# Hedgehog linear attention plus a Mish layer on one core: per-head weights loaded by rows and spread by TensorE, and a new order of the head of the program

## The chip, the cores and the metric

The kernel runs on one core of one Trainium2 chip. The metric is the device time of one execution in microseconds (us), as the median of several runs. Before the change it is 173.7 us: three runs gave 173.72, 173.63 and 173.70.

## What is computed

The input x has 2048 tokens of 512 features. Each token is normalised (layer norm without weights), and two branches start from the normalised tokens xn: a linear attention with 32 heads of 16 features, and a dense layer of 512 -> 1792 -> 512 with Mish. The result is x plus both.

```python
q, k, v = split_heads(xn @ wqkv)                 # 32 heads of 16
pq, pk  = q @ w_phi[h], k @ w_phi[h]             # 16 x 16 weights of each head
phi     = concat(softmax(p), softmax(-p))        # for q and for k
kv, z   = sum_s phi_k * v, sum_s phi_k
A       = ((phi_q @ kv) / (phi_q @ z + 1e-6)) @ wo
B       = mish(xn @ w1 + b1) @ w2
out     = x + A + B
```

## The kernel before

Everything is bf16 in SBUF; products go through PSUM, whose first six banks hold one 128x512 tile each. Tokens come in 16 tiles of 128, four to a group. Two weights of the attention are multiplied together on the chip first: the 512x512 weights of the keys, and w_phi as a block-diagonal matrix. The product, `wkp`, gives the logits pk from xn in one projection. That product is needed before the first logits can be made, so the head of the program (everything before the large stream of matmuls) has two strands that meet in `first_logits` (L197):

- Tokens: the first two tiles of x are loaded (L477), their mean and variance taken on VectorE (`first_stats`, L549), the inverse root made on GpSimd or on ScalarE (`first_root`, L553), the tile normalised on VectorE (`first_apply`, L562), turned by TensorE (`first_turn`, L566) and copied to `xnT` (`first_keep`, L587).
- Weights: the keys' weights come in two ways. Their last two blocks of 128 rows are turned by the DMA (L483, into `wT`). The first two are loaded as they are (L482, into `wkp`), turned on TensorE by matmuls with an identity (`turn_keys`, L573, tile `ptw`) and copied to `wT` by ScalarE (`keep_keys`, L581). w_phi is loaded into `wsrc` (L488) with row 16 i + a of a partition block holding row a of head i; a partition receives four runs of 16 elements. `weights_by_block` (L527) multiplies it with the mask `block` on VectorE to `Wbd`, the block-diagonal matrix. `fold` (L147) multiplies `wT` with `Wbd` into the tile `pfold`, four matmuls for each of the four blocks of 128 rows, and `unfold` (L159) copies each block to `wkp`.

`first_logits` takes the four blocks of `wkp` in order, each with both tiles of tokens (8 matmuls, tile `pl`). Behind it stands `value` (L209), the projection to v with the weights `wv`, and then the rest: logits of the other tokens, the hidden layer (`hidden`, L218), Mish on ScalarE (`mish`, L231), softmax work on VectorE and ScalarE, the key-value sums, the queries, the output.

The order of all work is written out by hand: `STEPS` (L24) is a list of short names with arguments, `run` (L627) maps each name to a function, and each engine executes its instructions in the order in which the steps issue them; semaphores make one engine wait for another. `H 3 @5` is hidden unit 3 into PSUM bank 5, `M 3` its Mish, `LC 0 2 a` the copy of a tile of logits by ScalarE, `v` stands for VectorE, `p` for GpSimd. The loads of the head stand in front of the list (L477 to L493) and go out on two queues: SyncE's (SP) and ScalarE's. Ahead of everything TensorE does 12 dummy matmuls on constants (L519), nine of 512 columns and three of 128; `WARM, SHORT = 9, 3`. GpSimd makes the constants: the identity `ident`, the mask `block`, `mhalf`, `eps` and the ones in `vext` (L496 to L508).

Of the kernel before, what the change touches and what calls it, by code (L numbers as in the profile page):

```python
# [22 lines left out]
WARM, SHORT = 9, 3  # L23
# [3 lines left out]
@4,5; LS 2; LS 3; RS 2 a; LC 0 0 a; V 1 @1; RS 3 p; AZ 2; TP 2 @2; TC 2 a; VC 1 a; AM; V 0 @3; LC 0  # L27
1 v; AZ 3; CB; TP 3 @4; TC 3 v; L 0 2 @5; LC 0 2 a; H 0 @0; M 0; L 0 3 @2; LC 0 3 a; H 1 @1; M 1; H
2 @4; M 2; H 3 @5; H 4 @0; H 5 @2; VC 0 a; H 6 @1; M 3; M 4; M 5; H 7 @4; M 6; M 7; H 8 @3; H 9 @5;
H 10 @0; M 8; H 11 @2; H 12 @1; LN 1; M 9; E 0 0; AP 1 0; AP 1 1; H 13 @4; L 1 0 @3; DX 3; L 1 3 @5;  # L30
DW 2; E 0 1; X 0 1; LN 2; LC 1 0 v; LC 1 3 v; WL 1; LN 3; AP 2 0; AP 2 1; X 0 0; V 6 @3; M 10; M 11;
M 12; H 14 @5; S 0 0; WL 2; LC 1 2 a; VC 6 a; M 13; AP 3 0; H 15 @0; H 16 @2; H 17 @1; LC 1 1 a; AP
3 1; WT; H 18 @3; H 19 @4; M 14; M 15; M 16; M 17; H 20 @5; M 18; M 19; H 21 @0; H 22 @2; H 23 @1; H
24 @3; M 20; M 21; H 25 @4; H 26 @5; M 22; M 23; H 27 @0; M 24; M 25; M 26; M 27; H 28 @2; M 28; H
29 @1; M 29; E 1 0; E 1 1; S 0 1; L 2 1 @3; L 2 0 @4; LC 2 0 v; L 2 2 @5; LC 2 1 v; L 2 3 @0; F 0
@2; R 0 0 a; L 3 2 @1; R 0 1 a; LC 2 2 v; LC 2 3 a; FC 0 a; X 1 0; F 1 @4; F 2 @3; FC 2 a; N 0 0; L
3 0 @5; V 9 @0; LC 3 0 a; V 3 @2; VC 3 a; LC 3 2 v; A 0 0; VC 9 a; V 7 @1; F 3 @3; V 2 @5; VC 7 a; V
8 @2; L 3 3 @0; FC 3 a; X 1 1; VC 2 a; FC 1 v; E 2 0; L 4 0 @4; DW 3; LC 3 3 a; E 2 1; V 4 @1; N 0
1; VC 8 v; X 2 0; S 1 1; LC 4 0 a; S 1 0; L 4 3 @3; VC 4 a; L 4 2 @5; V 11 @0; A 0 1; LC 4 2 a; V 5
@2; VC 11 a; R 1 1 a; S 2 0; L 4 1 @4; LC 4 1 a; L 3 1 @1; VC 5 a; LC 3 1 a; H 30 @5; H 31 @0; LC 4  # L40
3 v; R 1 0 a; M 30; H 32 @4; M 31; M 32; H 33 @2; M 33; N 1 1; H 34 @1; H 35 @3; H 36 @5; M 34; H 37
@0; M 35; H 38 @4; E 3 0; H 39 @2; H 40 @1; M 36; N 1 0; M 37; M 38; M 39; H 41 @3; H 42 @5; H 43
@0; M 40; A 1 0; M 41; E 3 1; M 42; M 43; A 1 1; X 2 1; V 12 @4; VC 12 a; L 5 0 @2; V 10 @1; V 15
@3; VC 15 a; V 13 @5; V 14 @0; E 4 0; E 4 1; LC 5 0 a; VC 13 v; VC 10 a; L 5 2 @4; X 3 1; X 3 0; L 6
3 @3; VC 14 a; L 5 3 @2; O 0 @5; LC 5 2 a; S 2 1; S 3 1; S 3 0; R 3 1 a; R 2 1 a; N 2 1; R 2 0 a; L
6 0 @1; R 3 0 a; N 3 0; L 5 1 @0; LC 5 1 a; N 3 1; O 1 @4; L 6 1 @0; LC 6 0 a; LC 6 3 a; L 6 2 @1; H
44 @3; X 4 0; N 2 0; S 4 0; LC 6 2 a; LC 6 1 v; LC 5 3 a; A 2 0; A 2 1; A 3 0; A 3 1; H 45 @1; X 4
1; M 44; W 4 0 v; H 46 @2; H 47 @0; M 45; M 46; S 4 1; M 47; KV; H 48 @3; M 48; H 49 @1; H 50 @2; M
49; H 51 @0; H 52 @3; M 50; M 51; Q 0 0; H 53 @1; G 0 0; H 54 @2; M 52; Q 0 1; H 55 @0; W 4 1 v; L 7
3 @3; M 53; M 54; E 5 0; G 0 1; L 7 0 @1; E 5 1; Q 1 0; C 0 a; O 2 @2; G 1 0; LC 7 0 a; X 5 0; Q 1  # L50
1; O 3 @1; G 1 1; E 6 0; S 5 0; P 0; P 1; C 1 a; LC 7 3 a; W 5 0 v; L 7 2 @3; M 55; Y 0; O 4 @0; O 5
@5; P 2; LC 7 2 a; Y 1; X 5 1; Q 2 0; G 2 0; L 7 1 @4; E 6 1; LC 7 1 a; P 3; S 5 1; Y 2; W 5 1 v; X
6 0; Q 2 1; G 2 1; O 6 @3; O 7 @2; E 7 0; C 2 a; S 6 0; Y 3; W 6 0 a; E 7 1; Q 3 0; O 8 @4; P 4; Y
4; G 3 0; X 6 1; Q 3 1; G 3 1; X 7 0; S 6 1; C 3 a; O 9 @1; P 5; X 7 1; W 6 1 v; Q 4 0; G 4 0; O 10
@0; Y 5; Q 4 1; G 4 1; S 7 0; C 4 a; O 11 @5; W 7 0 v; Q 5 0; G 5 0; P 6; P 7; Q 5 1; G 5 1; Y 6; O
12 @3; S 7 1; C 5 a; Q 6 0; W 7 1 a; P 8; P 9; G 6 0; Q 6 1; Y 7; Y 8; Y 9; G 6 1; O 13 @2; Q 7 0; C
6 v; G 7 0; P 10; P 11; Y 10; Q 7 1; O 14 @4; G 7 1; P 12; C 7 a; Y 11; Y 12; P 13; OH 0 @1; P 14;
PH 0; OH 1 @0; PH 1; Y 13; Y 14; YH 0; YH 1
# [4 lines left out]
def kernel(  # L63
# [29 lines left out]
    wphi_v = A_w_phi.rearrange("(j i) a b -> (i a) j b", j=4)  # L93
# [18 lines left out]
    wsrc = wts.tile([P, 4, DH], BF16, name="wsrc")  # L112
    wv = wts.tile([P, KT, D], BF16, name="wv")
# [8 lines left out]
    ident = consts.tile([P, P], BF16, name="ident")  # L122
    mhalf = consts.tile([P, TPG], FP32, name="mhalf")
# [9 lines left out]
    tables = ["natural_log_exp_and_others"]  # L133
# [343 lines left out]
    for t in range(2):  # L477
        nc.sync.dma_start(x_sb[:, t, :], x_v[:, t, :])  # L478
# [4 lines left out]
    nc.sync.dma_start_transpose(  # L483
        out=wT_of[0][:, :, 2 * P : 4 * P], in_=A_wqkv[2 * P : 4 * P, D : 2 * D]
    )
    nc.scalar.dma_start(b1b[:], b1_v[:, :])
    with nc.allow_non_contiguous_dma(reason="tiny w_phi load"):
        nc.scalar.dma_start(wsrc[:], wphi_v)  # L488
    nc.sync.dma_start(x_sb[:, 2:4, :], x_v[:, 2:4, :])
    nc.sync.dma_start(wv[:], wqkv_v[:, :, 2 * D : 3 * D])  # L490
    nc.sync.dma_start(w1_sb[:, :, 0 : 7 * P], w1_v[:, :, 0 : 7 * P])
    nc.sync.dma_start(x_sb[:, 4:8, :], x_v[:, 4:8, :])
    nc.sync.dma_start(w1_sb[:, :, 7 * P : F], w1_v[:, :, 7 * P : F])  # L493

    nc.scalar.preload_act_table_set(tables[0])
    make_identity(nc, ident[:])  # L496

    nc.gpsimd.memset(block[:], 1.0)
# [6 lines left out]
    nc.gpsimd.memset(mhalf[:], -0.5)  # L505
    nc.gpsimd.memset(eps[:], 1e-5)
# [12 lines left out]
    for n in (512,) * WARM + (P,) * SHORT:  # L519
        dummy(n)  # L520

# [5 lines left out]
    def weights_by_block():  # L527
        nc.vector.tensor_tensor(
            out=Wbd[:].rearrange("p j (h e) -> p j h e", h=8),
            in0=block[:, None, :, :].to_broadcast([P, 4, 8, 16]),  # L530
            in1=wsrc[:, :, None, :].to_broadcast([P, 4, 8, 16]),
            op=ALU.mult,
        )
# [19 lines left out]
    def first_root(i, on):  # L553
        _, mv, rstd = ln_of[0]
        r = rstd[:, i : i + 1]
        if on == "a":
            nc.scalar.activation(r, mv[:, i, 1:2], ACT.Ln, bias=eps[:])
            nc.scalar.activation(r, r, ACT.Exp, scale=-0.5)
        else:
            root(r, mv[:, i : i + 1, :])  # L560
# [26 lines left out]
    def first_keep(i, copy):  # L587
        copy(xnT[:, i, :, :], pf_of.pop(("t", i))[:].rearrange("p (k c) -> p k c", k=KT))
# [34 lines left out]
    def load_queries():  # L623
# [4 lines left out]
        "KM": masks, "AW": lambda: dummy(P), "WB": weights_by_block, "PB": bias,  # L628
# [52 lines left out]
```

## Time and profile before

| | us |
|---|---|
| median of three runs (lowest, highest) | 173.7 (173.63, 173.72) |
| span of the profiled execution, first to last instruction | 172.0 |
| the rest of the time, around the span | 1.7 |
| TensorE busy, of the span | 168.0 (98%) |
| VectorE busy | 143.9 (84%) |
| ScalarE busy | 123.8 (72%) |
| GpSimd busy | 7.8 (5%) |

The profile gives the profiled execution no time of its own beside its span, so the rest around the span is taken as the median less the span. All times inside the profile count from the start of that span. Engines are named PE (TensorE matmul), PEld (its weight loads), DVE (VectorE), ACT (ScalarE), POOL (GpSimd) and SP (the queue that issues most transfers). A row of the timeline has the start in us, the duration in us, the engine, the line and operation, the output and input, the shapes, how many instructions are merged in it (x2), and in brackets how long the engine stood idle before it and what ended that wait. Matmuls are pipelined: a row with eight of them lasts from the first one's start to the last one's end.

### The profile page before, as it was taken

To read this page: it belongs to the slowest core of one execution; us is meant where nothing else is said; L and a number is where in the kernel's file an instruction comes from. 1 tells how busy PE (TensorE), PEld (TensorE's weight loads), DVE (VectorE), ACT (ScalarE), POOL (GpSimd) and SP (SyncE) were. 2 spreads that over 40 slices of the span, in tenths; PEclk is the share of its full clock that TensorE was granted. 3 is DMA by queue.
4 is the path that set the end of the run, shared out by engine and by line. 5 is a ranking of instruction groups with operands and counts; after the bars stand their busy time and mean duration, and the time that the engine had idled before them with its cause. 6 is when DMAs were issued, how large, how long until landed. Compare 5 with 4: busy or idle time off the path is not lost.

```text
span 172.0 us, 2735 instructions
## 1 busy us (share of the span) xinstructions
PE 168.0 (98%) x1047; PEld 82.6 (48%) x1047; DVE 143.9 (84%) x223; ACT 123.8 (72%) x199; POOL 7.8 (5%) x23
## 2 busy tenths in 40 slices
PE   8899999999999999999999999999999999999993
PEld 2554444444454544454445644544444444554452
DVE  3869998999599999969989999799799998884333
ACT  2778899997999989889978989977282792432200
POOL 4123002300000000000000000000000000000000
PEclk9999999999999999999999999999999999999999
DMA  4997299589000000000000194309335618668941
GB/s 124 303 370 248 54 255 347 99 162 228 21 0 0 0 4 0 0 0 0 4 0 0 36 113 99 61 9 150 90 97 116 153 52 197 146 134 216 110 131 61
DMA packets 44185, 18.02 MB, mean 105 GB/s; under 512 B 35980, under 2 KB 44172, under 8 KB 44172
## 3 DMA queue, kind: packets, MB, share of 16 engines
q1 hardware_dynamic: 43472, 17.73, 43.9%
q8 instruction: 8, 0.13, 0.4%
q10 hardware_dynamic: 700, 0.12, 0.4%
q14 instruction: 5, 0.04, 0.1%
HBM read 7.10 MB, written 2.10 MB: 53 GB/s over the span
## 4 chain that ended last, share of the span: by engine, by line
PE 95%; DMA 2%; SPq 0%; ACT 0%; issue 0%; DVE 0%
PE po L457 28%; PE ph L223 28%; PE pl L189 14%; PE po L464 8%; PE pv L189 8%; PE pnd L412 2%; PE pkv L381 2%; DMA wkp<-in_A_wqkv_dram 2%; PE pl L204 1%; PE pfold L151 1%; PE pwide L189 1%; SPq L478 0%; PE ptr L569 0%; PE ptw L576 0%; ACT wT L582 0%
## 5 line engine op out<-in xcount | busy, mean ns | idle before, releaser
L457 PE MATMUL po<-w_sb,acts 128*128 128x512 bf16 (+2 forms) x238 | 50.8, 366 | 0.0
L223 PE MATMUL ph<-xnT,w_sb 128*128 128x512 bf16 x224 | 49.8, 379 | 0.0
L234 ACT ACTIVATE acts<-ph,b1f 128x512 bf16<-128x512 f32 x56 | 36.3, 701 | 4.2 <-PE ph L223 4.0
L300 DVE TENSOR_REDUCE s<-e 128x128 f32<-128x2048 bf16 x16 | 36.1, 2276 | 0.5 <-ACT e L283 0.5
L223 PEld LDWEIGHTS <-w_sb 128*128 128x128 bf16 x224 | 21.7, 98 | 25.7
L457 PEld LDWEIGHTS <-acts 128*128 128x128 bf16 x238 | 22.1, 98 | 23.6
L283 ACT ACTIVATE e<-e 128x2048 bf16<-128x2048 bf16 x16 | 30.5, 1919 | 0.0
L189 PEld LDWEIGHTS <-xnT 128*128 128x128 bf16 x184 | 17.5, 98 | 19.6
L471 DVE TENSOR_TENSOR x_sb<-po,x_sb 128x512 bf16<-128x512 f32 (+2 forms) x17 | 11.0, 656 | 8.4 <-PE po L464 8.4
L464 PE MATMUL po<-wqk,xnT 128*128 128x512 bf16 (+2 forms) x68 | 15.6, 366 | 0.0
L189 PE MATMUL pv<-wv,xnT 128*128 128x512 bf16 x64 | 15.6, 379 | 0.0
L189 PE MATMUL pl<-wqk,xnT 128*128 128x512 bf16 x64 | 15.4, 379 | 0.0
L427 ACT COPY ds<-pnd 128x32 f32<-128x32 f32 x16 | 2.9, 182 | 16.5 <-PE pnd L412 16.5
L247 ACT CAST p_sb<-pl 128x512 bf16<-128x512 f32 x21 | 12.2, 594 | 3.6 <-PE pl L189 3.4
L139 ACT ACT_TABLE_LOAD x10 | 12.8, 1283 | 0.2
L258 DVE TENSOR_TENSOR m<-m 128x512 bf16<-128x512 bf16 (+1 forms) x32 | 11.5, 359 | 1.1
L189 PE MATMUL pl<-wkp,xnT 128*128 128x512 bf16 x48 | 11.7, 379 | 0.0
L267 DVE TENSOR_TENSOR e<-p_sb,m 128x2048 bf16<-128x2048 bf16 x8 | 9.8, 1226 | 1.8 <-PE pkv L381 1.5
L258 DVE TENSOR_TENSOR m<-p_sb 128x1024 bf16<-128x1024 bf16 x16 | 10.9, 681 | 0.0
L165 DVE BATCH_NORM_STATS2 stats<-x_sb 128x6 f32<-128x512 bf16 x16 | 10.1, 677 | 0.9 <-DMA x_sb<-in_A_x_dram 0.9
L267 DVE TENSOR_TENSOR e<-m,p_sb 128x2048 bf16<-128x2048 bf16 x8 | 9.8, 1225 | 0.3
L334 DVE TENSOR_TENSOR e<-e,r 128x2048 bf16<-128x2048 bf16 x8 | 9.6, 1216 | 0.5 <-ACT r L309 0.5
(68 smaller groups left out, 133.9 us busy)
## 6 DMA issues: line engine op xcount, KB each, us to landing
w_sb<-in_B_w_dram SPq DMA_DIRECT2D x4, 896.0 KB, 7.8
out_dram<-x_sb SPq DMA_DIRECT2D x15, 128.0 KB, 1.8
x_sb<-in_A_x_dram SPq DMA_DIRECT2D x3, 512.0 KB, 7.5
wv<-in_A_wqkv_dram SPq DMA_DIRECT2D x1, 512.0 KB, 4.6
wqk<-in_A_wo_dram SPq DMA_DIRECT2D x1, 512.0 KB, 4.9
x_sb<-in_A_x_dram SPq DMA_DIRECT2D x2, 128.0 KB, 2.1
wkp<-in_A_wqkv_dram SPq DMA_DIRECT2D x1, 256.0 KB, 3.6
x_sb<-in_A_x_dram SPq DMA_DIRECT2D x1, 256.0 KB, 3.6
```

Source lines behind the costliest of these rows:

```text
L139: nc.scalar.preload_act_table_set(name)
L189: nc.tensor.matmul(pp, lhsT=xnT[:, t, kt, :], rhs=w[:, kt, :], start=(kt == 0), stop=(kt == KT - 1),)
L223: nc.tensor.matmul(ph_of[u][:], lhsT=w1_sb[:, kt, f * P : (f + 1) * P], rhs=xnT[:, g * TPG : (g + 1) * TPG, kt, :], start=(kt == 0), stop= ...
L234: nc.scalar.activation(acts[:, f, g * 512 : (g + 1) * 512], ph_of.pop(u)[:], ACT.Mish, bias=b1f[:, f : f + 1])
L247: copy(p_of[s][:, i, :], pl_of.pop((s, i)))
L258: nc.vector.tensor_tensor(out=m[:], in0=src[:, :, 0:half], in1=src[:, :, half : 2 * half], op=op)
L267: nc.vector.tensor_tensor(out=e_of[s][:].rearrange("p t j l c -> p (t j) l c")[:, :, pl, :].rearrange("p t (c e o) -> p t c e o", e=8, o=2 ...
L283: nc.scalar.activation(v, v, ACT.Exp)
L300: nc.vector.reduce_sum(t[:], pair(s, k).rearrange("p t j l (c e) -> p (t j l c) e", e=16), axis=AX.X)
L457: nc.tensor.matmul(po_of[t, c.stop][:, c], lhsT=acts[:, f, t * P : (t + 1) * P], rhs=w2_sb[:, f, c], start=(f == 0), stop=False,)
L464: nc.tensor.matmul(po_of[t, c.stop][:, c], lhsT=oT_of[t // 2][:, t % 2 * 4 + j, :], rhs=wo_sb[:, j, c], start=False, stop=(j == 3),)
L471: nc.vector.tensor_tensor(out=y, in0=po_of.pop((t, c.stop))[:, c], in1=y, op=ALU.add)
```

## The change

Five things change, all of them in the head.

1. w_phi is loaded by rows: `wraw` has in each partition four whole rows of 16 of one head, one run of 64 elements. A constant `sel`, a matrix of 0 and 1 kept in the memory of `kvm`, spreads them: 16 matmuls of 16 columns (`spread`) put the rows where `wsrc` has them, in a PSUM tile `pspread`, and VectorE copies that to `wsrc` (step `WC`).
2. The loads become steps (`D`), in a new order. ScalarE's queue carries the first tile of x and w_phi; SP's the second tile of x, the keys' weights in two loads of one block each, the turned blocks, tiles 2 and 3 of x, b1, and the rest. The third group's tokens go ahead of the second half of w1.
3. VectorE fills `ident`, `block`, `sel`, `eps` and `mhalf`; GpSimd only selects in them (`affine_select`).
4. The dummies become steps too (`AW`): five of 512 columns, one of 256 and two of 128 at the start, and two of 512 behind the turned keys' weights.
5. The steps of the head stand in another order, up to the first group's hidden units; from `H 13` on the list is as it was.

```diff
-KM; LS 0; RS 0 p; LS 1; RS 1 a; DX 2; PB @0; AZ 0; AZ 1; TW 0 @1; TW 1 @2; TP 0 @3; TP 1 @4; TK 0 a;
-TK 1 a; WB; F0 0 @5; FD 0 a; F0 1 @1; TC 0 v; F0 2 @2; F0 3 @3; FD 2 a; TC 1 v; FD 1 v; FD 3 a; LP i
+AW 512; AW 512; D x011 s; D wn01 s; AW 512; D wn12 s; AW 512; D x001 a; D phi a; AW 512; LS 0; AW
+256; AW 128; AW 128; WX @2; TL; TW 0 @1; RS 0 a; TK 0 a; TW 1 @4; LS 1; WC v; D wt1 s; AZ 0; KM; AW
+512; WB v; AW 512; D x022 s; RS 1 p; TP 0 @0; TK 1 a; F0 0 @5; AZ 1; TC 0 v; FD 0 a; F0 1 @2; TP 1
...
-    nc.sync.dma_start(wkp[:, 0:2, :], wqkv_v[:, 0:2, D : 2 * D])
-    nc.scalar.dma_start(b1b[:], b1_v[:, :])
-        nc.scalar.dma_start(wsrc[:], wphi_v)
...
+        elif what[:2] == "wn":
+            k = slice(int(what[2]), int(what[3]))
+            q.dma_start(wkp[:, k, :], wqkv_v[:, k, D : 2 * D])
...
+        elif what == "phi":
+            q.dma_start(wraw[:], A_w_phi.rearrange("h (c a) b -> (h c) (a b)", c=4))
...
+    nc.gpsimd.affine_select(
+        out=sel, in_=sel, pattern=[[1, 4 * P + 4]], compare_op=ALU.not_equal,
+        fill=1.0, base=-3, channel_multiplier=-4,
+    )
...
-    for n in (512,) * WARM + (P,) * SHORT:
-        dummy(n)
...
+    def spread(b):
+
+        pf_of["x"] = bank(b, "pspread")
+        for j in range(4):
+            for a in range(4):
+                nc.tensor.matmul(
+                    pf_of["x"][:, j * DH : (j + 1) * DH],
+                    lhsT=sel[:, j * P + 3 - a : (j + 1) * P + 3 - a],
+                    rhs=wraw[:, a * DH : (a + 1) * DH],
+                    start=(j == 0 and a == 0), stop=(a == 3), skip_group_check=True,
+                )
...
+        "WC": lambda c: copies[c](wsrc[:].rearrange("p j b -> p (j b)"), pf_of.pop("x")[:, 0 : 4 * DH]),
```

Three places show what the new list does to the engines.

VectorE between the statistics of the second tile and those of the third; before (`xn` is a normalised tile, `Wbd` the block-diagonal weights, `xnT` the turned tiles, `wkp` a block of the product):

```order
L167 BN_AGGR mv<-stats 128x2
L176 TENSOR_SCALAR xn<-x_sb,mv,rstd 128x512 x2
L528 TENSOR_TENSOR Wbd<-block,wsrc 128x512
L588 COPY xnT<-ptr 128x512 x2
L160 COPY wkp<-pfold 128x512
L165 BN_STATS stats<-x_sb 128x6
```

and the same stretch of VectorE now:

```order
L168 BN_AGGR mv<-stats 128x2
L653 COPY wsrc<-pspread 128x64
L177 TENSOR_SCALAR xn<-x_sb,mv,rstd 128x512
L534 TENSOR_TENSOR KVmask<-block 128x64
L551 TENSOR_TENSOR Wbd<-block,wsrc 128x512
L177 TENSOR_SCALAR xn<-x_sb,mv,rstd 128x512
L612 COPY xnT<-ptr 128x512 x2
L166 BN_STATS stats<-x_sb 128x6
```

The copy of the spread weights and the mask of the key-value sums came in, the block-diagonal weights moved ahead of the second normalised tile, and the copy of a block of `wkp` left.

ScalarE from its first instruction to the first tile of logits; before:

```order
L486 DMA b1b<-in_B_b_dram 14x128
L488 DMA wsrc<-in_A_w_phi_dram 128x4x16
L495 ACT_TABLE_LOAD
L557 ACTIVATE rstd<-mv,eps 128x1
L558 ACTIVATE rstd<-rstd 128x1
L582 COPY wT<-ptw 128x4x128 x2
L160 COPY wkp<-pfold 128x512 x3
```

and now:

```order
L485 DMA x_sb<-in_A_x_dram 128x512
L498 DMA wraw<-in_A_w_phi_dram 128x64
L140 ACT_TABLE_LOAD
L581 ACTIVATE rstd<-mv,eps 128x1
L582 ACTIVATE rstd<-rstd 128x1
L606 COPY wT<-ptw 128x4x128 x2
L161 COPY wkp<-pfold 128x512 x4
```

The first tile of x took the place of b1 on ScalarE's queue, the inverse root here is now the first tile's (it was the second's), and ScalarE copies all four blocks of `wkp` instead of three.

SP's queue from its first issue to the turned second group; before:

```order
L478 DMA x_sb<-in_A_x_dram 128x512 x2
L482 DMA wkp<-in_A_wqkv_dram 128x2x512
L483 DMA_TRANSPOSE wT<-in_A_wqkv_dram 128x4x256
L489 DMA x_sb<-in_A_x_dram 128x2x512
L490 DMA wv<-in_A_wqkv_dram 128x4x512
L491 DMA w_sb<-in_B_w_dram 128x4x896
L492 DMA x_sb<-in_A_x_dram 128x4x512
L493 DMA w_sb<-in_B_w_dram 128x4x896
L605 DMA x_sb<-in_A_x_dram 128x4x512
```

and now:

```order
L485 DMA x_sb<-in_A_x_dram 128x512
L490 DMA wkp<-in_A_wqkv_dram 128x512 x2
L493 DMA_TRANSPOSE wT<-in_A_wqkv_dram 128x4x256
L485 DMA x_sb<-in_A_x_dram 128x2x512
L500 DMA b1b<-in_B_b_dram 14x128
L487 DMA wv<-in_A_wqkv_dram 128x4x512
L496 DMA w_sb<-in_B_w_dram 128x4x896
L485 DMA x_sb<-in_A_x_dram 128x4x512
L629 DMA x_sb<-in_A_x_dram 128x4x512
L496 DMA w_sb<-in_B_w_dram 128x4x896
```

The keys' weights moved up by one transfer and are split in two, b1 came in ahead of the values' weights, and the third group's tokens moved ahead of the second half of w1.

More of the change, by code (lines that the diff above doesn't have):

```diff
@@ L6 @@
 from concourse._compat import with_exitstack
-from concourse.masks import make_identity
 BF16 = mybir.dt.bfloat16
@@ L30 @@
[L30 to L39, printed above, removed]
@@ new lines @@
+    nc.vector.memset(ident[:], 0.0)
+    nc.vector.memset(block[:], 1.0)
+    nc.vector.memset(sel, 0.0)
+    nc.vector.memset(eps[:], 1e-5)
+    nc.vector.memset(mhalf[:], -0.5)
+    nc.gpsimd.affine_select(
+        out=ident[:], in_=ident[:], pattern=[[-1, P]], compare_op=ALU.not_equal,
+        fill=1.0, base=0, channel_multiplier=1,
+    )
+    nc.gpsimd.affine_select(
+        out=sel, in_=sel, pattern=[[1, 4 * P + 4]], compare_op=ALU.not_equal,
+        fill=1.0, base=-3, channel_multiplier=-4,
+    )
```

99 lines of the change are left out of this document (56 added, 43 removed).

## The prediction

> **What bounds the kernel now.** I read the page first (TensorE is busy for nearly the whole span), then who waits for whom on TensorE (PE), then the chain of waits in order of time, then the head's timeline by engine and the transfers. The waits of TensorE over the whole span are two (engine and line, waited for: us in total, times, longest):
>
> ```profile
> PE warm L514 <- PEq L665: 0.8, 1, 0.8
> PE ptw L576 <- DMA wkp<-in_A_wqkv_dram: 0.4, 1, 0.4
> ```
>
> So after the second, at 5.4 us, TensorE never stands still for long. What the head hangs on is in the chain of waits (start, us, what), followed back from the end:
>
> ```profile
> 1.72 3.59 DMA wkp<-in_A_wqkv_dram
> ...
> 6.28 0.60 ACT wT L582
> ```
>
> Behind this copy the chain is TensorE alone: folds, logits, the values' projection, and so on to the end. From the projection on (`pv`, 9.39 below) matmul follows matmul, so the time is the moment at which it starts plus a fixed stream. **The question is how much earlier or later than 9.39 it starts, and whether the stream stays closed behind it.** The change leaves the stream's matmuls as they are.
>
> The head's timeline, first VectorE alone:
>
> ```profile
> 3.77 0.66 DVE L165 BATCH_NORM_STATS2 stats<-x_sb 128x6 f32<-128x512 bf16 x1
> 4.47 0.18 DVE L167 BATCH_NORM_AGGREGATE mv<-stats 128x2 f32<-128x6 f32 x1
> 4.87 0.85 DVE L176 TENSOR_SCALAR xn<-x_sb,mv,rstd 128x512 bf16<-128x512 bf16 x2 [0.22 <-POOL rstd L172]
> 5.64 0.42 DVE L528 TENSOR_TENSOR Wbd<-block,wsrc 128x512 bf16<-128x512 bf16 x1
> 6.24 0.76 DVE L588 COPY xnT<-ptr 128x512 bf16<-128x512 bf16 x2 [0.18 <-PE ptr L569]
> 7.36 0.69 DVE L160 CAST wkp<-pfold 128x512 bf16<-128x512 f32 x1 [0.36 <-PE pfold L151]
> ```
>
> then ScalarE alone, and two rows of TensorE:
>
> ```profile
> 4.75 0.29 ACT L557 ACTIVATE rstd<-mv,eps 128x1 f32<-128x1 f32 x1 [1.55 <-DVE mv L167]
> 5.08 0.20 ACT L558 ACTIVATE rstd<-rstd 128x1 f32<-128x1 f32 x1
> 5.79 1.07 ACT L582 CAST wT<-ptw 128x512 bf16<-128x512 f32 x2 [0.51 <-PE ptw L576]
> 6.87 1.78 ACT L160 CAST wkp<-pfold 128x512 bf16<-128x512 f32 x3
> ```
>
> ```profile
> 6.43 1.33 PE L151 MATMUL pfold<-Wbd,wT 128*128 128x128 bf16 x16
> ...
> 9.39 1.03 PE L189 MATMUL pv<-wv,xnT 128*128 128x512 bf16 x4
> ```
>
> The folding of the weights starts at 6.43, just behind ScalarE's first copy of the turned keys' weights (from 5.79 to 6.38); these had waited for their load until 5.31 (1.72 + 3.59). The logits then wait for the copy on VectorE (7.36 + 0.69 = 8.05) and run to 9.39.
>
> The transfers of the head (KB each, us from issue to landing):
>
> ```profile
> wv<-in_A_wqkv_dram SPq DMA_DIRECT2D x1, 512.0 KB, 4.6
> x_sb<-in_A_x_dram SPq DMA_DIRECT2D x2, 128.0 KB, 2.1
> wkp<-in_A_wqkv_dram SPq DMA_DIRECT2D x1, 256.0 KB, 3.6
> wsrc<-in_A_w_phi_dram ACTq DMA_DIRECT2D x1, 16.0 KB, 4.0
> wT<-in_A_wqkv_dram SPq DMA_TRANSPOSE x1, 4.2
> w_sb<-in_B_w_dram SPq DMA_DIRECT2D x2, 896.0 KB, 9.4
> ```
>
> **The change part by part.**
>
> *Loads.* w_phi came as four runs of 32 bytes a partition, 512 pieces, and took 4.0. It now comes as 128 pieces of 128 bytes, behind one tile of x on ScalarE's queue. The nearest rows are a tile of x (128 pieces, 2.1) below and the old load (4.0) above:
>
> ```profile
> 0.78 0.66 ACTq L486 DMA_DIRECT2D b1b<-in_B_b_dram  x1
> 1.47 0.41 ACTq L488 DMA_DIRECT2D wsrc<-in_A_w_phi_dram  x1
> 2.19 1.32 SPq L483 DMA_TRANSPOSE wT<-in_A_wqkv_dram  x1
> 4.17 0.46 SPq L490 DMA_DIRECT2D wv<-in_A_wqkv_dram  x1
> 5.78 0.51 SPq L493 DMA_DIRECT2D w_sb<-in_B_w_dram  x1
> ```
>
> Issued at 1.2 to 1.5, it lands between 3.4 and 5.5. I take 3.5, by the number of pieces. The keys' weights are two loads of 128 KB, issued at about 1.25 and 1.7: like a tile of x they land at 3.4 and 3.8; the upper end for the second block is the old landing, 5.3. I take 3.4 and 3.9. The first two tiles of x go out at 0.8 on two queues instead of 0.8 and 1.24 on one, and I leave their landing as it was.
>
> *Constants.* GpSimd's select of 128 columns:
>
> ```profile
> 1.06 0.29 POOL masks.py:199 TENSOR_SCALAR_AFFINE_SELECT ident<-ident 128x128 bf16<-128x128 bf16 x1
> ```
>
> `sel` is 516 columns, at most four times 0.29 = 1.2, behind `ident`, so it is ready by about 2.6; the wait for w_phi (3.4 at the earliest) covers it. VectorE's five fills fall before its first tile of x, where it is idle. Cost nothing; without that cover, the excess over 3.5 one to one.
>
> *Spread.* 16 matmuls of 16 columns. The nearest row is this one, with 68 columns:
>
> ```profile
> 152.27 0.26 PE pnd L412 x8
> ```
>
> 0.033 each, 0.53 in all; twice that, 1.05, while the clock is still at half (see the rivals). From 3.58, with the clock rising at about 4.3 as before: done at 4.45, in PSUM at 4.65. If each cost as much as a 128-column matmul (1.33 for 16 overlapped, some 0.07 each), it would be 0.3 more.
>
> *VectorE.* The second tile's statistics end at 4.65 (4.47 + 0.18). There VectorE stood 0.22 waiting for GpSimd's root; the first root is now ScalarE's, which takes 0.29 + 0.20. Two more of its rows, the mask and the copy of b1:
>
> ```profile
> 2.37 0.22 DVE L523 TENSOR_TENSOR KVmask<-block 128x64 f32<-128x64 bf16 x1 [2.37 <-POOL block L500]
> 11.07 0.17 DVE L629 CAST b1f<-pb 128x14 f32<-128x14 bf16 x1
> ```
>
> ScalarE's root follows the first tile's statistics (they end before 3.77 + 0.1) and ends at about 4.5. The copy of the spread weights is 64 columns, a little over the 0.17 of the 14-column copy: 0.22, and it goes into the old wait. The first normalised tile starts at 4.83 (it was 4.87). Then come the mask (0.22, from 5.15) and `Wbd` (0.42, from 5.30): ready at 5.72 instead of 6.06, because the second normalised tile, 0.42, is now behind it. That tile then ends at 6.08, it was 5.72; its turning and copy end at 7.06 instead of 7.00, which only the second logits matmul reads.
>
> *Keys.* Turning ends at 4.75 instead of 5.81; ScalarE's two copies take 1.07 from 4.9 and end at 6.0 instead of 6.86. The first fold therefore waits for `Wbd`, not for a copy: 5.77 instead of 6.43. The turned half (issue 2.19, landing 6.4) is in time for the third fold at 6.45.
>
> *Unfold.* A fold's copy starts 0.44 behind it (6.43 to 6.87): 6.21. All four are on ScalarE now, 0.48 apart (two take 1.07, one 0.59 to 0.60 by the chain): the last ends at 6.21 + 3 x 0.48 + 0.59 = 8.24. The last two logits matmuls follow, 0.05 and 2 x 0.216 later (L223: 46 in 10.09):
>
> ```profile
> 14.16 10.09 PE L223 MATMUL ph<-xnT,w_sb 128*128 128x512 bf16 x46
> ```
>
> so the projection could start at 8.73.
>
> *The values' weights.* They land at 4.17 + 4.6 = 8.8 before, covered until 9.39. With that cover gone they end last: start at 8.88. They may land a little earlier (fewer small pieces ahead) or later (b1 ahead of them on SP).
>
> *What lies behind.* VectorE takes over copies of 128x512 from ScalarE between the projection and the next group's statistics: two of values and one more of logits, at 0.69 each (the price of its copy at 7.36), for a turned tile that it gives away. Bounds for those statistics: 0.5 earlier, if the copies fit into gaps, and 3 x 0.69 - 0.5 = 1.6 later. What follows from the later end:
>
> ```profile
> 19.13 2.63 SPq L181 DMA_TRANSPOSE xnT<-xn  x2
> 25.38 1.89 PE L189 MATMUL pl<-wkp,xnT 128*128 128x512 bf16 x8
> xnT<-xn SPq DMA_TRANSPOSE x1, 3.2
> ```
>
> The next group's turned tokens land at 19.13 + 3.2 + 1.6 = 23.9 at the latest; TensorE asks for them at 25.4 - 0.5 = 24.9. The second half of w1 is moved past 512 KB of tokens, 1.4 at the 377 GB/s of the row under the third rival; it landed at 5.78 + 9.4 = 15.2 and so lands near 16.6. Hidden unit 9, its first user, comes 11.5 matmul groups of 0.86 (4 x 0.216) after the projection's start, near 18.8. Both covers hold, by 1.0 and 2.2; if one is gone, the excess counts one to one.
>
> **Sum.** 9.39 - 8.88 = 0.51 less, against the execution's span of 172.0 and the 1.7 around it: 171.5 + 1.7 = 173.2. If the values' weights land 0.25 earlier, the logits decide, 0.66 less: 173.0.
>
> **The rivals.**
>
> *The clock rises late (slower).* The dummies of before:
>
> ```profile
> L514 PE MATMUL warm<-const-bfloat16-1.0 128*128 128x512 bf16 x9 | 3.8, 607 | 0.8 <-PEq L665 0.8
> L514 PE MATMUL warm<-const-bfloat16-1.0 128*128 128x128 bf16 x3 | 0.3, 221 | 0.0
> ```
>
> Nine of 512 columns take 3.8, 0.42 each, against 0.216 later; the three short ones already run at full speed. So the clock was at half until TensorE had been busy for 3.5 us. The new dummies end at 0.83 + 5 x 0.42 + 0.42 = 3.4, and a gap of some 0.2 follows. If that gap starts the count anew, the clock rises near 7.1. Then the serial work up to the first fold is at half speed: spread 1.05, turned keys 0.9, two dummies 0.85, first turned tile 0.45, fold 0.45, 3.7 from 3.58, 7.28 instead of 6.0. The copies shift by 1.3, the projection starts at 10.0, 0.6 later than before: 174.3. It decides once the clock rises after about 5.4, since a microsecond at half speed costs half. For it: the dummies are 1.4 shorter. Against: the gap is 0.2 in 3.5, and the work that follows it is dense until 4.75. [...]
>
> *w_phi lands late (slower).* If 128-byte pieces were no quicker than the old load, it lands at 5.5 and the chain 3.58 to 8.73 moves with it, shorter by some 0.3 at full clock: 10.3, 174.6. Even at 4.55. Against: a quarter of the pieces.
>
> *The values' weights land later (no change).* With b1's issue (0.66) ahead of theirs and a landing that follows the issue, 4.17 + 0.66 + 4.6 = 9.4: 173.7. For it: their landing decides in the forecast too. Against: the transfers' share in the windows is full, so landing goes by bytes ahead, which are the same:
>
> ```profile
> 8.00:9.30 1.30, 1.30 (x7) 0.58 (x6) 1.27 (x4) 1.02 (x4) 0.00 (x0) 1.00 1.05 377
> ```
>
> (last two columns: share of the DMA engines, GB/s).
>
> **How the numbers follow.** Forecast 173.2 with chance 0.62, from 172.9 (both landings early) to 173.35; a smaller gain or none through the values' weights 0.21; the clock 0.10; w_phi 0.06; something unseen 0.01. 0.2% is 0.35 us, about what a measurement of this kernel can tell from no change. Faster by more than that is the forecast and a sliver of the second case, 0.64; within it 0.20; slower 0.16, the two late cases. The range 172.9 to 174.1 takes in the second case and the milder half of the late clock.
>
> **What would show it.** In the profile after: the first fold near 5.8 and bound by `Wbd`; the last copy of `wkp` on ScalarE near 8.2; the values' projection near 8.9 with a short wait for their load; no TensorE wait behind it; span 171.5. The spread's matmuls start at w_phi's landing: near 3.6 if I am right on it, near 5.5 if the second rival is. Short matmuls 0.11 apart behind 4.5 would show the late clock. I am wrong if TensorE waits anywhere behind the projection, or if the span ends where it did although the projection starts earlier.

## The result, and the profile after

The change made the kernel slower: 175.22 us (median of 6 runs, 174.38 to 175.80) against 173.66 (6 runs, 173.40 to 174.08), a ratio of 1.0085 with a 95% interval of 1.0063 to 1.0107. The runs also scatter twice as far as before, over 1.4 us.

The profiled execution took 174.91, its span is 173.2. That is 0.31 less than the median, so what follows explains the profiled execution; the slower ones left no profile. TensorE's waits over the whole span are again two (waited for: us in total, times, longest):

```profile
PE warm L528 <- PEq L691: 0.8, 1, 0.8
PE pspread L543 <- DMA wraw<-in_A_w_phi_dram: 0.5, 1, 0.5
```

So TensorE never waits behind the head, and yet the time is longer. TensorE's timeline of the head shows where:

```profile
0.82 2.72 PE L528 MATMUL warm<-const-bfloat16-1.0 128*128 128x512 bf16 x8 [0.82 <-PEq L691]
4.07 0.60 PE L543 MATMUL pspread<-wraw,kvm 128*128 128x16 bf16 x16 [0.53 <-DMA wraw<-in_A_w_phi_dram]
4.52 1.05 PE L600 MATMUL ptw<-ident,wkp 128*128 128x128 bf16 x8
5.36 1.06 PE L528 MATMUL warm<-const-bfloat16-1.0 128*128 128x512 bf16 x2
6.21 0.63 PE L593 MATMUL ptr<-ident,xn 128*128 128x128 bf16 x4
6.64 1.06 PE L152 MATMUL pfold<-Wbd,wT 128*128 128x128 bf16 x8
...
8.60 1.89 PE L205 MATMUL pl<-wkp,xnT 128*128 128x512 bf16 x7
10.33 1.03 PE L190 MATMUL pv<-wv,xnT 128*128 128x512 bf16 x4
...
12.60 0.18 PE L560 MATMUL pb<-ident,b1b 14*128 14x14 bf16 x1
12.70 1.04 PE L190 MATMUL pl<-wkp,xnT 128*128 128x512 bf16 x4
```

The projection starts at 10.33, 0.93 later than before, where 8.88 was forecast. The first fold starts at 6.64, not 5.77, and eight turning matmuls of 128 columns take 1.05. The last matmul ends the stream 1.15 later: 0.93 of the projection and 0.2 of `pb` (b1's turn), which now stands in the stream and holds it up between its two neighbours. The chain of waits (start, us, what) runs from w_phi's landing over TensorE alone, and the two dummies behind the keys are a link of it:

```profile
1.21 2.83 DMA wraw<-in_A_w_phi_dram
...
5.57 0.85 PE warm L528 x2
6.42 0.43 PE ptr L593 x4
6.85 0.85 PE pfold L152 x8
```

The matmuls of the head grouped by shape, from 4.0 to 8.4 (times, busy us, mean ns of one):

```profile
L152 PE MATMUL pfold<-Wbd,wT 128*128 128x128 bf16 x13 | 1.7, 308 | 0.0
L593 PE MATMUL ptr<-ident,xn 128*128 128x128 bf16 x8 | 1.3, 314 | 0.0
L528 PE MATMUL warm<-const-bfloat16-1.0 128*128 128x512 bf16 x2 | 1.1, 634 | 0.0
```

The same groups of the kernel before, from 4.0 to 8.0:

```profile
L151 PE MATMUL pfold<-Wbd,wT 128*128 128x128 bf16 x16 | 1.2, 220 | 0.1
L569 PE MATMUL ptr<-ident,xn 128*128 128x128 bf16 x8 | 0.6, 219 | 0.0
```

A fold of 128 columns shows 308 ns where it showed 220, and the starts lie 107 ns apart instead of 56 until 8.3: half clock. Before, the full clock came at 4.35. VectorE's rows (start, us, what) show a second loss that is no matter of the clock:

```profile
3.67 0.70 DVE L166 BATCH_NORM_STATS2 stats<-x_sb 128x6 f32<-128x512 bf16 x1 [2.25 <-DMA x_sb<-in_A_x_dram]
...
5.85 0.42 DVE L551 TENSOR_TENSOR Wbd<-block,wsrc 128x512 bf16<-128x512 bf16 x1
6.74 0.41 DVE L177 TENSOR_SCALAR xn<-x_sb,mv,rstd 128x512 bf16<-128x512 bf16 x1 [0.47 <-POOL rstd L173]
```

The first statistics start at 3.67; in the profile before they started at 2.95. The second tile is normalised from 6.74, behind GpSimd's root. Beside the clock there are two more causes to test: the landing of the first tiles of x, and b1's turn.

### The profile page after: what moved, and what is told of

Its sections match the earlier page's. It is cut to its first block, busy times and chain, and to the rows that moved or that the text cites. A ratio compares the mean times of both kernels' runs of the same rounds, so it can differ in the third digit from the quotient of the medians.

```text
span 173.2 us, 2752 instructions
## 1 busy us (share of the span) xinstructions
PE 168.3 (97%) x1046; PEld 84.4 (49%) x1061; DVE 145.6 (84%) x231; ACT 122.0 (70%) x197; POOL 8.4 (5%) x20
## 4 chain that ended last, share of the span: by engine, by line
PE 96%; DMA 2%; issue 1%; ACTq 0%; DVE 0%
PE ph L224 28%; PE po L458 28%; PE pl L190 14%; PE po L465 8%; PE pv L190 8%; PE pnd L413 2%; PE pkv L382 2%; DMA wraw<-in_A_w_phi_dram 2%; PE pfold L152 1%; PE pwide L190 1%; PE pl L205 1%; PE ptr L593 1%; PE ptw L600 1%; PE warm L528 0%; PE pspread L543 0%
## 5 line engine op out<-in xcount | busy, mean ns | idle before, releaser
L235 ACT ACTIVATE acts<-ph,b1f 128x512 bf16<-128x512 f32 x56 | 35.3, 704 | 4.8 <-PE ph L224 4.6
L248 ACT CAST p_sb<-pl 128x512 bf16<-128x512 f32 x20 | 11.6, 595 | 4.8 <-PE pl L190 4.3
```

The lines of the kernel that those rows point to most:

```text
L235: nc.scalar.activation(acts[:, f, g * 512 : (g + 1) * 512], ph_of.pop(u)[:], ACT.Mish, bias=b1f[:, f : f + 1])
L248: copy(p_of[s][:, i, :], pl_of.pop((s, i)))
```

## Experiments

Every kernel was timed beside the kernel before on the same chip. The table gives the times ("own" is the time of the execution that was profiled), and from each kernel's one profile the moment at which the clock went full (from the trace's record of the clock; for the changed kernel's first profile from the spacing of its matmuls), the start of the first statistics and of the projection, in us. Kernels 2, 6 and 11 are the kernel before with one part changed, the others the changed kernel. In the edits, `D x001 s` loads from tile 0 of x one tile on SyncE's queue (`a`: on ScalarE's), `D wn01` a block of the keys' weights, `D wv` the values' weights; `WX` is the spread, `PB` and `CB` b1's turn and its copy, `TL` the load of ScalarE's table.

```
kernel                    median  (range)            ratio to before [95%]   own     clock  stats  projection
before (first profile)    173.66  (173.40 to 174.08)                         173.7    4.35  2.95   9.39
changed                   175.22  (174.38 to 175.80) 1.0085 [1.0063, 1.0107] 174.91   8.4   3.67  10.33
e1  longer dummies        174.66  (174.40 to 174.82) 1.0049 [1.0030, 1.0068] 174.56   4.11  3.30   9.36
e2  before, short dummies 174.87  (173.70 to 175.41) 1.0054 [1.0029, 1.0078] 175.19   9.94  2.87  10.89
e3  other loads           175.28  (173.61 to 175.77) 1.0070 [1.0044, 1.0095] 174.44   6.68  2.90   9.84
e4  both                  174.35  (174.01 to 175.13) 1.0042 [1.0028, 1.0057] 174.96   6.68  2.86   9.79
e5  longer, same count    174.35  (173.78 to 175.11) 1.0034 [1.0017, 1.0051] 173.90   5.83  3.33   9.31
e6  before, more matmuls  173.89  (173.45 to 174.68) 1.0012 [0.9994, 1.0030] 173.64   4.83  2.91   9.31
e7  b1 in the head        174.70  (173.95 to 175.31) 1.0055 [1.0033, 1.0077] 173.95   6.11  3.60   9.58
e8  wv on ScalarE's queue 175.41  (174.98 to 176.27) 1.0096 [1.0072, 1.0120] 176.27   5.16  3.47  10.55
e9  changed, again        174.92  (174.05 to 175.53) 1.0070 [1.0046, 1.0095] 174.05   4.88  3.48   9.47
e10 wv in halves          174.16  (173.70 to 174.41) 1.0024 [1.0013, 1.0034] 173.91   4.48  3.46   9.45
e11 before, spread alone  174.87  (174.64 to 175.10) 1.0065 [1.0052, 1.0079] 175.04   6.44  2.97   9.87
e12 tiles of x on SP      173.99  (173.78 to 175.78) 1.0039 [1.0013, 1.0065] 174.16   4.98  2.96   9.17
```

**1 to 4: clock or loads.** Theory A makes the late clock the larger loss, rival B the later landing of the loads. In e1 the dummies reach to w_phi's landing; e2 gives the kernel before the short dummies; e3 issues the loads otherwise; e4 is e1 and e3 together.

```
e1  -AW 256; AW 128; AW 128; WX @2;
    +AW 512; AW 512; AW 512; AW 128; AW 128; WX @2;
e2  -for n in (512,) * WARM + (P,) * SHORT:
    +for n in (512,) * 5 + (256, P, P):
e3  -D x011 s; D wn01 s; D wn12 s; D x001 a; D phi a; ... D b1 s;
    +D x001 s; D x011 s; D wn01 s; D wn12 s; D phi a; D b1 a;
```

> The changed kernel with longer dummies (seven of 512 columns and two of 128 in place of five of 512, one of 256 and two of 128), so that TensorE is busy until about 4.0 and the gap ahead of the spread (0.5 us in the changed kernel) is closed. Nothing else differs. Theory A (the gap held the clock at half until 8.3, and this is the larger part of the loss): short matmuls 56 ns apart from about 4.4 on, the values' projection at 9.4 to 9.7 instead of 10.32, the time 174.0 to 174.3 (0.6 to 0.9 below the changed kernel). Rival B (the loads land later, and TensorE's speed in the head hardly counts): the clock may rise early, but the projection stays at 10.2 to 10.4 and the time at 174.9 to 175.2.

> The kernel before with only its dummies cut to those of the changed kernel (five of 512, one of 256, two of 128 columns instead of nine of 512 and three of 128). Theory A: with TensorE idle from 3.5 to 5.3 the clock stays at half to 8 us or beyond; turning, folds and the first logits run at half speed, the projection starts at 10.0 to 10.4 instead of 9.39, the time is 174.3 to 174.7. Rival B: the head is paced by loads and copies, the projection stays at 9.4 to 9.5, the time at 173.7.

> The changed kernel with its short dummies, but the head's loads issued otherwise: both first tiles of x on SP again, w_phi first on ScalarE's queue and b1 behind it there, so that it leaves SP's queue ahead of the values' weights. The first statistics should start near 2.95 instead of 3.66, w_phi land near 3.3 instead of 4.03. Rival B (the landings are the larger part): the projection at 9.3 to 9.6, the time 173.8 to 174.2. Theory A (the clock is): a gap ahead of the spread remains or shrinks little, the clock stays at half to 7 us or beyond, the projection at 9.9 to 10.3, the time 174.5 to 175.0. If w_phi lands so early that the gap closes, the clock tells: then it must rise near 4.4 and the time fall to about 173.6.

> Both edits together: the loads issued otherwise and the longer dummies. Theory A with B as a smaller part: clock full from about 4.4, the projection at 9.0 to 9.3, the time 173.4 to 173.8 (0.2 of it is the turn of b1, which stays in the stream). Theory A alone (landings don't count): as the kernel with longer dummies alone, 174.0 to 174.3. Rival B alone: as the kernel with the other loads alone.

e1's TensorE in the head and at the end (start, us, what):

```profile
4.67 0.61 PE L599 MATMUL ptw<-ident,wkp 128*128 128x128 bf16 x8
...
9.36 1.04 PE L189 MATMUL pv<-wv,xnT 128*128 128x512 bf16 x4
```

```profile
158.15 0.43 PE L412 MATMUL pnd<-kvm,qT 128*128 128x68 bf16 x8 [0.43 <-DMA qT<-e]
```

The turning takes 0.61, not 1.05, and the projection starts at 9.36, a little ahead of theory A's 9.4 to 9.7. Not all of that is the clock, since tile and w_phi also landed 0.4 and 0.2 earlier. The time, 174.66, is outside A's range: a stall appeared near the end (second fence: a wait of 0.43, which makes the stream 0.6 longer), which neither theory had. e2 is the cleanest case for A: the kernel before, with nothing altered but its dummies, has TensorE waiting 1.3 for the keys, and what follows at half clock up to the fourth of eight logits matmuls (groups, then two rows of the timeline):

```profile
L151 PE MATMUL pfold<-Wbd,wT 128*128 128x128 bf16 x16 | 1.9, 314 | 0.0
L576 PE MATMUL ptw<-ident,wkp 128*128 128x128 bf16 x8 | 1.0, 311 | 1.3 <-DMA wkp<-in_A_wqkv_dram 1.3
```

```profile
8.40 2.66 PE L204 MATMUL pl<-wkp,xnT 128*128 128x512 bf16 x8
10.89 1.03 PE L189 MATMUL pv<-wv,xnT 128*128 128x512 bf16 x3
```

Its clock went full at 9.94, its projection started 1.5 late (A had 10.0 to 10.4, too little), its median rose by 0.54% (0.29 to 0.78), to 174.87. Rival B, which had it unchanged, falls as the whole story.

e3 does not decide between the two. It brought the statistics to 2.90 and w_phi to 3.03; the gap was then behind the spread (0.44, for the keys), and the clock went full at 6.68. Its last logits matmul started at 9.34, so that the projection could have followed near 9.55, in B's range of 9.3 to 9.6. It came at 9.84, because the values' weights landed only then (its chain of waits):

```profile
4.64 5.16 DMA wv<-in_A_wqkv_dram
...
9.84 1.04 PE pv L189 x4
```

Its runs lie from 173.61 to 175.77, their median of 175.28 above both ranges. e4 missed: it had no gap, and its clock still went full at 6.68 only, its projection at 9.79, its median at 174.35 instead of 173.4 to 173.8. A gap was not all that decides.

**5 to 8: the stall at the end, b1, the values' weights.** e5 is e1 with two matmuls fewer, e6 the kernel before with 16 more; e7 adds to e5 b1's turn in the head; e8 adds to that the values' weights on ScalarE's queue, x's tiles swapped, and dummies shorter by 256 columns.

```
e5  -AW 256; AW 128; AW 128; WX @2;
    +AW 512; AW 512; AW 256; WX @2;
e6  -for n in (512,) * WARM + (P,) * SHORT:
    +for n in (512,) * 4 + (P,) * 22 + (64,) * 2:
e7  -D phi a; ... WB v; AW 512; ... D b1 s; ... PB @4; ... CB;
    +D phi a; D b1 a; ... WB v; PB @3; CB;
e8  -D x011 s; ... D x001 a; ... TL; ... D wv s;
    +D x001 s; ... D x011 a; ... TL; D wv a;
```

> The changed kernel with longer dummies (seven of 512 columns, one of 256), but as many instructions on TensorE as it has (the kernel with seven of 512 and two of 128 had two matmuls more). That kernel showed the projection at 9.35 and a new stall of 0.6 us at 157.4: the turned e tile landed late, while a 16 KB fetch on queue q8 (TensorE's instructions) ran at 155.9; in the changed kernel this fetch came at 160.6, behind the last such tile. Theory F (the place of the fetch moves with the count of TensorE's instructions and holds up the tile): no stall at 157.4, the fetch behind 159, the time 173.8 to 174.1 (the projection near 9.35, 0.2 for b1's turn). Rival (the stall comes from the earlier start, or by chance of the transfers): the stall is there again, 174.5 to 174.8.

> The kernel before with its dummies cut into smaller ones: four of 512, twenty-two of 128 and two of 64 columns in place of nine of 512 and three of 128, the same columns in all, 16 matmuls more, so that TensorE has as many instructions as the kernel that showed the stall at 157.4. Nothing else differs. Theory F: the last fetch of instructions comes near 155.5 instead of 159.1, TensorE stalls near 157.4 for some 0.6, the time is 174.1 to 174.4. Rival: the head is as before and so is the time, 173.6 to 173.8.

> The changed kernel with the longer dummies (seven of 512, one of 256), b1 loaded third on ScalarE's queue instead of on SP's ahead of the values' weights, its turn on TensorE back in the head (in place of one of the two dummies behind the keys' turning) and its copy behind the block weights. If the turn of b1 in the stream costs 0.2 and its issue on SP holds the values' weights back by 0.5: these land near 8.8 instead of 9.3 to 9.5, the projection starts at 8.9 to 9.2, the stream behind it is as long as before (159.7), and the time is 173.2 to 173.5 where the clock rises early. Rival (neither counts): 173.8 to 174.1 as the kernel with longer dummies alone.

> As the last, and: the first tile of x on SP and the second on ScalarE's queue (they were crossed, and the first to be used came last), the values' weights on ScalarE's queue behind its table load (issued near 3.2), and the dummies shorter by 0.2 (six of 512, two of 256) so that they end when w_phi lands. If loads and clock are all that was lost, the values' weights no longer end last, the projection starts at 8.7 to 9.0 and the time is 173.0 to 173.3, faster than the kernel before (173.66). If the values' weights now delay the tokens and the other loads behind them, TensorE waits further on, and the time is 173.6 or more.

The stall first. A row of the queues of e1's transfers from 155.5 to 157.5 (packets, MB, share), with the issue of the e tile that TensorE stalled for (us to landing), and behind them the same tile's issue in the kernel before:

```profile
q8 instruction: 1, 0.02, 3.9%
...
qT<-e SPq DMA_TRANSPOSE x1, 4.9
```

```profile
qT<-e SPq DMA_TRANSPOSE x1, 2.7
```

e1 fetches 16 KB of instructions there; the kernel before does that at 159.1, when its last turned e tile has landed. Behind the fetch some two dozen packets of 256 bytes took 1.3 to 1.6 us instead of 0.02, and the tile's 16 parts landed between 156.2 and 158.1. e5, with two matmuls fewer, has its last fetch at 157.45, earlier than theory F's 159, but no stall, and 173.90 in its profile, in F's range of 173.8 to 174.1; its median, 174.35, is not. e6 has the fetch at 155.74, as F said, and its packets stand likewise from 156.39 on, but its tile had landed at 156.09, and TensorE did not stall in the profile, against F. Seven of its 12 runs lie from 173.45 to 173.94, five from 174.19 to 174.68; whether those five stalled is not shown. The last fetch starts at 155.74 to 156.63 in the four kernels with e1's number of matmuls (e1, e4, e6, e11), and at 157.45 or later in the other ten. So its place does move with the number of TensorE's instructions, and in e6 0.3 us separated it from a stall. e4 and e11 stalled in the same way, and their streams were longer by 0.6 and 0.9.

b1's turn: e5 (first fence) has it in the stream, e7 (second) in the head:

```profile
11.26 0.39 PE L592 MATMUL ptr<-ident,xn 128*128 128x128 bf16 x4
11.57 0.18 PE L559 MATMUL pb<-ident,b1b 14*128 14x14 bf16 x1
11.68 1.04 PE L189 MATMUL pl<-wkp,xnT 128*128 128x512 bf16 x4
```

```profile
11.53 0.39 PE L592 MATMUL ptr<-ident,xn 128*128 128x128 bf16 x4
11.75 1.03 PE L189 MATMUL pl<-wkp,xnT 128*128 128x512 bf16 x4
```

From the turned tile to the next logits 0.42 against 0.22; from the projection's start to the last matmul's e5 takes 159.91 and e7 159.70, as before the change. That term is settled: 0.2. e7's projection was not earlier (9.58 instead of 8.9 to 9.2): its clock came at 6.11 and its tile of x late, 3.60, and taking b1 off SP's queue brought the values' weights in at 9.24, not at 8.8; its median is 174.70, above both ranges. e8 failed: the values' weights, issued at 3.64 on the second queue, landed at 10.51 (KB, us from issue to landing; then TensorE's waits):

```profile
wv<-in_A_wqkv_dram ACTq DMA_DIRECT2D x1, 512.0 KB, 6.9
```

```profile
PE ptr L592 <- DVE xn L176: 1.0, 2, 0.8
PE pv L189 <- DMA wv<-in_A_wqkv_dram: 0.9, 1, 0.9
```

In one load on SP they took 4.2 to 5.2 in the other profiles. Issued 0.5 to 1.3 earlier on the second queue they landed later, and they were not alone: tiles 2 and 3 of x, issued on SP at the same moment, took 6.7 instead of 3.4 to 4.3, and TensorE waited 0.8 more for the first of them.

**9 to 12: one kernel, two clocks; the tiles of x.** e9 is the changed kernel unaltered. e10 is e5 with b1 in the head, x's first tile on SP and second on ScalarE's queue, and the values' weights in halves; e12 is e10 with both tiles on SP and the keys' second block on ScalarE's queue. e11 puts the spread and VectorE's constants alone into the kernel before.

```
e10 -D wv s;
    +D wv02 s; D wv24 s;
e12 -D x001 s; D wn01 s; D wn12 s; D x011 a; D phi a;
    +D x001 s; D x011 s; D wn01 s; D phi a; D wn12 a;
e11 -PB @0; AZ 0; ... WB;
    +PB @0; WX @4; AZ 0; ... WC v; WB v;
```

> The changed kernel once more, unaltered, for a second profile. In the profiles so far the clock rises at moments that differ from run to run (4.1, 5.2, 5.8, 6.1, 6.7 and 6.7 with longer dummies or other loads, 8.4 in the first profile of the changed kernel, 9.9 with the short dummies in the kernel before), and the records of full clock last 48, 49 or 50 times 3.413 us. Theory A (the clock is decided in windows of 3.413 us whose start is not tied to the kernel's; a window that holds the gap ahead of the spread is lost, and the next decides): a rise either before 4.6 or between 7.9 and 10.2, and the projection follows it, near 9.4 for the early and 10.2 to 10.9 for the late rise. The times of the runs scatter over more than 1 us again, 174.0 to 175.8. Rival (the gap itself restarts a count, as in the prediction's rival, so that the rise always comes at one moment): 8.4 again, the projection at 10.3.

> The changed kernel with longer dummies (seven of 512, one of 256), b1 third on ScalarE's queue and its turn and copy in the head, the first tile of x on SP and the second on ScalarE's queue, and the values' weights in two loads of half the rows on SP, so that the projection's first two matmuls wait for the first half alone. If their landing is what holds the projection at 9.3 where the clock is early: the projection at 8.9 to 9.1, the stream behind it 159.7, the time 173.2 to 173.4. Rival (the clock's lottery and the copies hold it as well): the projection at 9.3 or later, the time 173.7 to 174.5, no gain over the kernel before.

> The kernel before with one part of the change alone: w_phi loaded by rows, spread by the 16 selection matmuls behind its long dummies, and the constants by VectorE; loads, dummies, roots and the order of the head as before. The prediction costed this part at nothing beside the loads. If that holds: the spread runs from about 4.7 to 5.1 at full clock, the folds start near 6.4 and the projection near 9.4, the time 173.5 to 173.9. Rival (the spread or the constants cost time by themselves): the block weights are ready after 6.4, the projection at 9.6 or later, 173.9 or more.

> The kernel with the values' weights in halves (longer dummies, b1 in the head), and both first tiles of x on SP's queue again, w_phi first and the second block of the keys' weights next on ScalarE's queue. In the profiles with one tile of x on each queue the first statistics started at 3.30 to 3.66, in those with both on SP at 2.86 to 2.97. If this half microsecond is the second term of the loss: statistics from 2.95, the block weights ready near 5.6 instead of 6.1, the second tile normalised from 6.0 instead of 6.5, the projection at 8.9 to 9.2 where the clock rises before 4.6, the time 173.4 to 173.7, at or below the kernel before. Rival (the clock's moment and the values' weights set it whatever the tiles do): the projection at 9.4 or later, 173.9 to 174.3.

e9 prices the clock. The changed kernel's second profile has full clock from 4.88; its folds take 219 ns instead of 308, its projection starts at 9.47 instead of 10.33, and it took 174.05 instead of 174.91. w_phi and the first tile of x landed 0.2 earlier too, so by this pair the clock alone costs 0.67 to 0.86:

```profile
L152 PE MATMUL pfold<-Wbd,wT 128*128 128x128 bf16 x16 | 1.2, 219 | 0.0
```

4.88 was in neither of theory A's ranges, so its rule that a window holding the gap is lost is too strict (last section); its rival, that the rise always comes at 8.4, fell too. With the clock early, what is left is in e9's chain of waits (start, us, what):

```profile
0.78 2.68 DMA x_sb<-in_A_x_dram
3.46 0.02 issue
3.48 0.71 DVE stats L166
...
4.39 0.59 DVE stats L166
...
5.28 0.39 POOL rstd L172
...
5.74 0.80 POOL rstd L173
...
6.56 0.43 DVE xn L177
...
7.03 0.40 PE ptr L593 x4
7.43 0.45 PE pfold L152 x8
7.88 0.68 PE pl L205 x3
```

The late tile of x, then the second tile's root on GpSimd, then the turning of that tile, and behind it, in TensorE's order, the last two folds and all logits. e12 has its tiles on SP's queue: statistics at 2.96 instead of e10's 3.46, and the projection at 9.17 instead of 9.45, with the clock full at 4.98 and 4.48:

```profile
2.96 0.69 DVE L165 BATCH_NORM_STATS2 stats<-x_sb 128x6 f32<-128x512 bf16 x1 [1.54 <-DMA x_sb<-in_A_x_dram]
```

```profile
9.17 1.03 PE L189 MATMUL pv<-wv,xnT 128*128 128x512 bf16 x4
```

That is the only projection clearly earlier than before's. TensorE no longer waits for the second tile there, as it did for 0.19 in e10. It did not pay, since the first hidden unit now came ahead of its weights:

```profile
PE ph L223 <- DMA w_sb<-in_B_w_dram: 0.4, 1, 0.4
```

By the stream this cost 0.55 in all, and the last matmul came 0.33 later than before's; the median, 173.99, is in the rival's range. e10 (the halves) kept its stream at 159.73 but its projection at 9.45, held by the chain above and not by the values' weights: its first expectation fails.

e11 missed as well, 174.87 where 173.5 to 173.9 was expected. Its spread runs from 5.20, behind the full dummies and b1's turn, and the keys' turning from 5.64 instead of 5.36; its clock came at 6.44 although the twelve dummies are those of the kernel before, and it had the stall at the end (0.9). By this profile the spread is free only ahead of the keys' landing; what each of these cost it does not show.

No kernel here is faster than the one before; e6 alone can't be told from it.

## Why the prediction was wrong

The forecast was 173.2, from a projection at 8.88; it came at 10.33, and the time, 175.22, outside the range of 172.9 to 174.1. By its own steps:

**The clock** is the step that failed most. The prediction let it rise "at about 4.3 as before" and gave the late rise a chance of 0.10. It rose at 8.4, and the one kernel seen with both clocks puts 0.67 to 0.86 us on that (10.33 to 9.47; up to 0.19 of it can be its tile of x and its w_phi, which also landed 0.2 earlier in e9). The two dummies that were to keep TensorE busy behind the keys took 0.85 of the chain at half clock. The rival's mechanism was right in kind (first fold done at 7.28 foretold, 6.64 + 0.43 = 7.07 measured; projection 10.0 foretold) and wrong in the detail that the gap restarts a count: with the same dummies the clock rose at 4.88 in e9 (last section). Nor did "as before" name a fixed moment: the dummies of the kernel before stand unaltered in e11, and there it rose at 6.44. What spoke against it in the text, that the gap was 0.2, rested on w_phi landing at 3.5; it landed at 4.03, and the gap was 0.53.

**The landing of the first tiles of x** was left "as it was". With them on two queues the first statistics began at 3.30 to 3.67 in seven profiles, on one queue at 2.86 to 2.97 in seven. With the late start `Wbd` was ready at 6.27 instead of 5.72.

**The second tile** was dismissed with "which only the second logits matmul reads". Its turning stands ahead of the third fold in TensorE's order, and its root, now GpSimd's 0.38 and 0.79, was not costed. It was ready at 7.15 in the changed kernel, 6.97 in e9, against 6.08 in the forecast. e9's and e10's chains run through it, and with tiles 0.5 earlier e12's projection came 0.28 earlier, though e12 also moved a block of the keys' weights. The root's own share is only argued, since no run put it back on ScalarE.

**b1's turn** in the stream was not costed at all: 0.2, shown by e7 against e5.

**The values' weights** landed at 9.52, later than forecast (8.8) and near the third rival's 9.4; in e1, e5 and e9, which issue them alike, at 9.31, 8.98 and 9.14, and in e3 at 9.80, where the projection waited for them. The rival's reason, b1's issue ahead of them, is not borne out: without it they landed at 9.24 in e7. So without the other losses the projection could have started at about 9.05 at best, a gain of 0.3 and not 0.51, and b1's turn takes 0.2 of it.

Right were: the selection and the constants on VectorE cost nothing (`sel` took 0.62, not 1.2, and was ready at 2.1); the spread took 0.45, even at half clock, where 0.53 and 1.05 had been worked out; the four copies on ScalarE took 2.05 to 2.11 where they ran in one row (2.03 foretold); and nothing waits behind the projection, neither for the next tokens nor for the second half of w1. The first half of w1, which the text did not look at, is what stopped TensorE once the projection came earlier (e12).

In sum: -0.51 forecast, +0.86 between the two profiles of the changed kernel, and +0.59 for tiles, root and order with the values' weights (9.47 against 8.88) make the projection's +0.94, and 0.2 for b1's turn gives the last matmul's +1.15. The 0.59 is what is left over and was not measured part by part. The median rose by 1.56; what the slower executions lost beyond the profiled one stays open.

## What to carry to other kernels

Work that only keeps TensorE busy is part of the schedule (the dummies cut alone cost 0.54% in e2): before shortening it, ask what stands in for it, and read several executions, since one profile shows one beginning of the full clock (from 4.11 to 9.94 in the fourteen here, 8.4 and 4.88 in the two of the changed kernel). An instruction that waits on an in-order engine delays all that is queued behind it, whoever reads its result (in e9 the turning of the second tile started at 7.03, and two folds and all logits came behind it); list that queue before calling a late tile harmless. When the head gets shorter, look up the next load of each stage, not only the last (in e12 TensorE waited 0.38 for the first half of w1).

## What the runs showed of the hardware

**The full clock lasts multiples of 3.413 us.** The stretches of full clock in the record are 163.84, 167.25 and 170.67 us, that is 48, 49 and 50 times 3.413 (the kernel before has 167.25), and they begin anywhere between 4.1 and 9.9. That the clock is decided in windows of 3.413 is the author's reading of these lengths; no record shows a window by itself. By that reading the profiles tell how much idleness a window at half clock bears. Counting back from each rise in windows of 3.413, with the time in which no matmul streams (the spread's short matmuls, 28 ns apart, count as one piece; the changed kernel's rise is from the spacing of its matmuls, since its trace has no record of the clock):

```
window that ends at the rise             window ahead of it (clock stayed at half)
before   0.93 to 4.35  idle 0.00         3.31
changed  4.99 to 8.40  idle 0.02         1.57 to 4.99  idle 0.79
e1       0.70 to 4.11  idle 0.13
e2       6.53 to 9.94  idle 0.00         3.11 to 6.53  idle 1.66
e3       3.27 to 6.68  idle 0.61         -0.14 to 3.27 idle 0.97
e4       3.27 to 6.68  idle 0.00         -0.15 to 3.27 idle 0.97
e9       1.47 to 4.88  idle 0.72         2.77
```

In all fourteen profiles, of the windows up to the rise those with up to 0.72 idle were followed by full clock and those with 0.79 or more by half. By this reading e4's clock was late because its window began 0.97 ahead of its first matmul. By it too the changed kernel and e9 have nearly the same phase (rises at 8.40, or 4.99 one window earlier, and at 4.88), and w_phi 0.2 earlier or later decided. The limit is read from these fourteen after the fact and not tested by itself, and its place depends on the count: with the pauses between the spread's matmuls as idle it lies between 0.95 (e9) and 0.97 (e3 and e4). It does not hold once the clock is full: the window behind the rise of the kernel before has over 1.1 idle, and the clock stayed.

**A fetch of instructions can hold up a transfer.** The 16 KB fetch on queue q8 took 0.88 to 1.72 us in the kernel before and the changed one, and where it met a turning transfer, packets of 256 bytes, 0.02 in the median, stood for 1.0 to 2.1 us, in the kernel before too (at 159.5, behind its last e tile); in e1, e4 and e11 TensorE waited for such a transfer (0.43, 0.42 and 0.71). From 30 us on the profiles of the kernel before and of the changed kernel hold 55 and 53 packets of 256 bytes that took over 1 us, and every one of them started within 1.2 us of the start of such a fetch. In the other eleven profiles TensorE has no wait for it; in these three it cost 0.6 to 0.9.

**A load on a second queue can be late.** The values' weights took 6.9 us there (e8), and 4.2 to 5.2 in one load on SP. With the first two tiles of x on two queues work on the first began at 3.30 to 3.67, with both on SP at 2.86 to 2.97, whichever of the two tiles was on ScalarE's queue (e8 and e10 have them swapped). Why it is so no run here tests by itself.
